# Issuing TensorE's matmuls block by block, and outer-product units that use all four row quadrants, in a fused attention and MLP backward kernel

## The chip, the cores and the metric

One core of a Trainium2 chip. The metric is the device time of one execution in microseconds (us). Executions of one kernel scatter; each is fast or slow (slow: more than 1.5% above the fastest of the same kernel), and ratios use fast runs alone.

## The reference

One token for two sequences goes through a layer norm, then in parallel through attention over a cache (32 query heads, 16 key and value heads, 4096 positions, head size 128) and a bilinear MLP (576 to 4608 and back). The function returns the output and all gradients. What matters here are the two largest of these, the gradients of the caches, each of the shape of the cache:

```python
def _fwd_reference(A_x, A_k_cache, A_v_cache, A_wq, A_wo, B_x, B_w_gate, B_w_up, B_w_down):
    # [...] _A_ref: scores = q k^T * Dh**-0.5, softmax, p v, times wo;  _B_ref: (x w_gate) * (x w_up) w_down
    x = A_x
    xn = _layernorm(x, axis=-1)
    return x + _A_ref(xn, A_k_cache, A_v_cache, A_wq, A_wo) + _B_ref(xn, B_w_gate, B_w_up, B_w_down)

def reference(...):            # [...]
    _out, _vjp = jax.vjp(_f, A_x, A_k_cache, A_v_cache, A_wq, A_wo, B_w_gate, B_w_up, B_w_down)
    return (_out, *_vjp(grad_out))
```

With one query position, the gradient of a cache row is a rank-one product: a row of 4096 numbers (probabilities, or gradients of scores) times a vector of 128. So the kernel reads 92 MB, writes 92 MB, and TensorE (PE) does many small matmuls.

## The kernel before

A framework records the instructions, and its scheduler decides at build time in which order they stand on each engine; PE ran its list in that order (its changes of array shape, counted in the traces and in the orders as built, are the same 683 before and 1010 after). PE uses its array in three shapes here: whole (128 rows x 128 columns, the scores), column tiles (128 x 32, contractions and the small MLP products), and row tiles (32 x 128, the outer products, whose contracted dimension is 32 rows of one row quadrant).

```python
    def ps_o():                                   # a pair tile, in two halves; two such tiles exist
        return ps.tile([P, 2, 512], FP32, tag="o", bufs=2, name="ps_o")

    def head_scores(n, t, x, s_ps, half):         # 16 whole-array matmuls on one half of a head
        # [...] a 32x32 transpose of half a head on DVE into X
        for e in range(2):
            be = 2 * half + e
            for c8 in range(8):
                nc.tensor.matmul(s_ps[:], lhsT=view(W[t][:], ...), rhs=view(X[:], ...), start=..., stop=...)

    def outer_units(rows, bd, b, l0, oview):      # gradients of two cache heads: 8 units, 256 in all
        def unit(x, ch, A):
            def f():
                # [...]
                o = ps_o()
                for c in range(4):
                    for aa in range(2):
                        a = 2 * A + aa            # row quadrant: 0 and 1, or 2 and 3
                        nc.tensor.matmul(o[:, aa, c * Dh:(c + 1) * Dh], lhsT=rows[32 * a:32 * a + 32, 4 * ch + c, :],
                                         rhs=bd[32 * a:32 * a + 32, x * Dh:(x + 1) * Dh], start=True, stop=True)
                evac(st[:, 2 * A:2 * A + 2, 4 * ch:4 * ch + 4, :].rearrange(...), o[:], 1024)
                # [...] the last unit of a head issues its 1 MB output DMA
            return f
        return [unit(x, ch, A) for x in range(2) for ch in range(2) for A in range(2)]
```

`evac` copies a tile from PSUM to SBUF as bf16, on ACT or DVE by a running account of their loads. The main loop mixes these units with the work on the next heads and with units of the MLP.

## Time and profile before

| | before |
|---|---|
| time, median of the first 3 runs | 550.38 us |
| PE, DVE, ACT busy (profiled run, slow, 560.2 us) | 475.7, 362.0, 330.6 us |
| mean granted clock of PE (profiled run; fast runs of later calls 0.78 to 0.82) | 0.766 |
| read and written | 92.48 and 92.48 MB |
| changes of array shape, in PE's order | 654 |

"Busy" of PE counts the modelled duration of every matmul; overlapping ones count once. Distances between starts say more, and the prediction works with them. The lines of the profile are shown there. The granted clock in the traces of the kernel before and of the changed one is either full (1.0) or half (0.5), and each record of it but the cut-off last lasts a whole multiple of 3.413 us, the shortest 3.413 us; a stretch of that length is called a window here, and the kernel before has 80 of them at full clock and 76 at half.

### The profile page before, as it was taken

To read this page: it belongs to the slowest core of one execution; us is meant where nothing else is said; L and a number is where in the kernel's file an instruction comes from. 1 tells how busy PE (TensorE), PEld (TensorE's weight loads), DVE (VectorE), ACT (ScalarE), POOL (GpSimd) and SP (SyncE) were. 2 spreads that over 40 slices of the span, in tenths; PEclk is the share of its full clock that TensorE was granted. 3 is DMA by queue.
4 is the path that set the end of the run, shared out by engine and by line. 5 is a ranking of instruction groups with operands and counts; after the bars stand their busy time and mean duration, and the time that the engine had idled before them with its cause. 6 is when DMAs were issued, how large, how long until landed. Compare 5 with 4: busy or idle time off the path is not lost.

```text
span 560.2 us, 20059 instructions
## 1 busy us (share of the span) xinstructions
PE 475.7 (85%) x8921; PEld 362.5 (65%) x8921; DVE 362.0 (65%) x624; ACT 330.6 (59%) x454; POOL 204.6 (37%) x372
## 2 busy tenths in 40 slices
PE   0588988998989999888989899998888999879873
PEld 0476766776776677666767667776776757767630
DVE  8685655757657646458575675668676646577564
ACT  1135695857566465567565665667555566566553
POOL 5125252432622521624235243344243243351322
PEclk9988798877787555688787975589888566798955
DMA  8993999999699998699997999979979889764546
GB/s 254 411 385 135 355 412 368 397 381 405 227 403 393 384 366 324 213 388 379 353 391 253 417 415 375 393 279 411 392 294 390 356 291 403 283 239 171 219 152 245
DMA packets 52911, 186.26 MB, mean 333 GB/s; under 512 B 4140, under 2 KB 19128, under 8 KB 44632
## 3 DMA queue, kind: packets, MB, share of 16 engines
q1 hardware_dynamic: 28392, 92.49, 44.3%
q0 software_dynamic: 24432, 92.48, 43.0%
q8 instruction: 70, 1.15, 0.8%
q14 instruction: 17, 0.14, 0.1%
HBM read 92.48 MB, written 92.48 MB: 330 GB/s over the span
## 4 chain that ended last, share of the span: by engine, by line
PE 31%; ACT 9%; issue 5%; DVE 4%; POOL 2%; POOLq 0%; DVEq 0%; ACTq 0%
PE ps_sc L503 11%; ACT so L93 8%; PE ps_o L549 6%; PE ps_m L518 4%; PE ps_m L527 1%; POOL prm L533 1%; PE ps_m L440 1%; PE ps_o L681 1%; DVE so L90 1%; PE ps_o L651 1%; DVE sto L90 1%; PE ps_m L272 1%; PE ps_o L364 1%; PE ps_m L618 1%; DVE X L102 1%
## 5 line engine op out<-in xcount | busy, mean ns | idle before, releaser
L93 ACT CAST so<-ps_o 128x1024 bf16<-128x1024 f32 x232 | 225.1, 1019 | 125.5 <-PE ps_o L549 114.0
L503 PE MATMUL ps_sc<-X,W 128*128 128x128 bf16 x2048 | 197.2, 249 | 5.3 <-DVE X L102 4.5
L102 DVE STREAM_TRANSPOSE X<-kv 128x1024 f32<-128x1024 f32 x128 | 157.6, 1233 | 44.1 <-PE ps_sc L503 42.7
L503 PEld LDWEIGHTS <-W 128*128 128x128 bf16 x2048 | 153.1, 112 | 27.7 <-issue 17.5
L553 POOL DMA_DIRECT2D out_dram<-so x64 | 50.0, 781 | 138.5 <-ACT so L93 74.6
L549 PE MATMUL ps_o<-bd,dsm 32*128 32x128 bf16 x1024 | 50.9, 245 | 10.3 <-ACT so L93 5.8
L518 PE MATMUL ps_m<-kv,rowT 128*32 128x128 bf16 x2048 | 59.3, 272 | 0.0
L549 PE MATMUL ps_o<-bd,prm 32*128 32x128 bf16 x1024 | 46.3, 250 | 14.3 <-POOL prm L533 7.0
L518 PEld LDWEIGHTS <-rowT 128*32 128x32 bf16 x2048 | 43.0, 121 | 10.0 <-issue 5.8
L549 PEld LDWEIGHTS <-dsm 32*128 32x128 bf16 x1024 | 30.4, 104 | 24.8 <-issue 18.4
L549 PEld LDWEIGHTS <-prm 32*128 32x128 bf16 x1024 | 27.8, 105 | 26.8 <-issue 13.5
L533 POOL TENSOR_TENSOR prm<-pr,maskc 128x1024 bf16<-128x1024 bf16 x16 | 30.2, 1888 | 36.5 <-DVE pr L580 36.5
L93 ACT CAST stw<-ps_o 128x1024 bf16<-128x1024 f32 x28 | 27.8, 1028 | 13.8 <-PE ps_o L364 12.6
L474 POOL COPY dM<-qd 128x128 bf16<-128x128 bf16 x32 | 9.3, 289 | 73.1 <-PE ps_m L480 46.2
L90 DVE CAST so<-ps_o 128x1024 bf16<-128x1024 f32 x24 | 29.1, 1211 | 8.7 <-PE ps_o L549 8.2
L467 POOL COPY W<-rep 32x16 bf16<-32x16 bf16 x128 | 24.7, 193 | 26.1 <-PE ps_sc L503 18.9
L533 POOL TENSOR_TENSOR dsm<-ds,maskc 128x1024 bf16<-128x1024 bf16 x16 | 30.2, 1889 | 4.6 <-DVE ds L600 4.0
L93 ACT CAST std<-ps_o 128x576 bf16<-128x576 f32 x36 | 22.8, 646 | 12.6 <-PE ps_o L397 12.4
L102 DVE STREAM_TRANSPOSE Xw<-wgu 128x1152 f32<-128x1152 f32 x18 | 24.5, 1360 | 4.1 <-PE ps_sc L503 4.0
L93 ACT CAST sto<-ps_o 128x576 bf16<-128x576 f32 x25 | 15.6, 642 | 14.1 <-PE ps_o L681 13.9
L719 DVE TENSOR_SCALAR oT<-ps_m 128x4 bf16<-128x4 f32 x16 | 2.7, 171 | 29.6 <-PE ps_m L527 29.6
L371 POOL DMA_DIRECT2D out_dram<-stw x18 | 13.5, 752 | 19.0 <-ACT stw L93 10.6
(178 smaller groups left out, 591.8 us busy)
## 6 DMA issues: line engine op xcount, KB each, us to landing
out_dram<-so POOLq DMA_DIRECT2D x64, 1024.0 KB, 9.5
kv<-in_A_k_cache_dram SPq DMA_DIRECT2D x32, 1024.0 KB, 11.8
kv<-in_A_v_cache_dram SPq DMA_DIRECT2D x32, 1024.0 KB, 10.1
out_dram<-stw POOLq DMA_DIRECT2D x18, 512.0 KB, 9.3
wd<-in_B_w_down_dram SPq DMA_DIRECT2D x9, 576.0 KB, 12.7
out_dram<-std POOLq DMA_DIRECT2D x9, 576.0 KB, 7.9
wo<-in_A_wo_dram SPq DMA_DIRECT2D x4, 1152.0 KB, 13.4
wgu<-in_B_w_gate_dram SPq DMA_DIRECT2D x9, 512.0 KB, 14.0
```

Of the source, the lines that this page charges most:

```text
L90: nc.vector.tensor_copy(out=out, in_=in_)
L93: nc.scalar.copy(out, in_)
L102: nc.vector.transpose(out, in_)
L272: nc.tensor.matmul(dp[32 * gq:32 * gq + 32, 0:P], lhsT=view(Wm[:], 0, P, 8 * pos(q, s), [[1, 32]]), rhs=view(X[:], 0, P, koff(s) * 256 + ( ...
L371: nc.gpsimd.dma_start(out[0:512, f0:f0 + FS].rearrange("(c p) n -> p c n", p=P), st[:])
L467: nc.gpsimd.tensor_copy(view(W[t][:], 32 * a, 32, 28 + 32 * a, [[2 * WW, 4], [WW + 2, 2], [1, 2]]), view(st["rep"][:], 32 * a, 32, t * 4 * ...
L474: nc.gpsimd.tensor_copy(view(dM[:], 0, P, t * 2 * P, [[P + 2, 2], [4, 32], [1, 2]]), view(st["qd"][:], 0, P, (2 if t == 0 else 1) * GH * 2 ...
L503: nc.tensor.matmul(s_ps[:], lhsT=view(W[t][:], 0, P, (be * 2 + x) * WW + 28 - 4 * c8, [[1, P]]), rhs=view(X[:], 0, P, c8 * 64 + e, [[8 * 6 ...
L518: nc.tensor.matmul(o_ps[32 * cg:32 * cg + 32, :], lhsT=view(rowsT[:], 0, P, c4 * 32 + 4 * c8, [[1, 32]]), rhs=head[:, 8 * c4 + c8, :], sta ...
L533: nc.gpsimd.tensor_tensor(m[:], view(rows[:], 0, P, 0, [[0, 8], [1, P]]), view(maskc[:], 0, P, 0, [[1, 8], [0, P]]), ALU.mult)
L549: nc.tensor.matmul(o[:, aa, c * Dh:(c + 1) * Dh], lhsT=rows[32 * a:32 * a + 32, 4 * ch + c, :], rhs=bd[32 * a:32 * a + 32, x * Dh:(x + 1) ...
L553: nc.gpsimd.dma_start(oview[b, :, :, l0 + x].rearrange("a m n -> m a n"), st[:].rearrange("p a c d -> p a (c d)"))
```

## The change

The intent is that PE runs one product after the other without a break, and that an outer-product unit keeps all four row quadrants at work. A class `Block` wraps each loop of matmuls. In the units of the caches, two units become one that fills both pair tiles, with the quadrants in the order 2, 0, 3, 1; the calls that hand out units are halved. Cut to its core:

```diff
+    class Block:
+        def __init__(self):
+            self.first, self.stack = None, ExitStack()
+        def __enter__(self):
+            return self
+        def __call__(self, *args, **kwargs):
+            ins = nc.tensor.matmul(*args, **kwargs)
+            if self.first is None:
+                self.first = ins
+                self.stack.enter_context(tc.issue_after(ins.ins))
+                self.stack.enter_context(tc.high_priority())
+        def __exit__(self, *exc):
+            self.stack.close()
 [...]
-        for e in range(2):
-            be = 2 * half + e
-            for c8 in range(8):
-                nc.tensor.matmul(
+        with Block() as mm:
+            for e in range(2):
+                be = 2 * half + e
+                for c8 in range(8):
+                    mm(
 [... the same around fifteen other loops of matmuls ...]
-        def unit(x, ch, A):
+        def unit(x, ch):
 [...]
-                o = ps_o()
-                for c in range(4):
-                    for aa in range(2):
-                        a = 2 * A + aa
-                        nc.tensor.matmul(o[:, aa, c * Dh:(c + 1) * Dh], lhsT=rows[32 * a:32 * a + 32, 4 * ch + c, :],
-                                         rhs=bd[32 * a:32 * a + 32, x * Dh:(x + 1) * Dh], start=True, stop=True)
-                evac(st[:, 2 * A:2 * A + 2, 4 * ch:4 * ch + 4, :].rearrange("p a c d -> p a (c d)"), o[:], 1024)
+                o = [ps_o(), ps_o()]
+                with Block() as mm:
+                    for c in range(4):
+                        for a in (2, 0, 3, 1):
+                            mm(o[a // 2][:, a % 2, c * Dh:(c + 1) * Dh], lhsT=rows[32 * a:32 * a + 32, 4 * ch + c, :],
+                               rhs=bd[32 * a:32 * a + 32, x * Dh:(x + 1) * Dh], start=True, stop=True)
+                for A in range(2):
+                    evac(st[:, 2 * A:2 * A + 2, 4 * ch:4 * ch + 4, :].rearrange("p a c d -> p a (c d)"), o[A][:], 1024)
```

`issue_after` only says that an instruction stands somewhere behind the block's first one on PE. `high_priority()` without a number sets the scheduler's count back to 0 for what is recorded inside.

More of the change, by code (lines that the diff above doesn't have):

```diff
@@ L268, in dxn @@
             dve(1.4)
-            for r in range(4):
-                for gq in range(4):
-                    q, s = 2 * half + gq // 2, 4 * (gq % 2) + r
-                    nc.tensor.matmul(
-                        dp[32 * gq:32 * gq + 32, 0:P], lhsT=view(Wm[:], 0, P, 8 * pos(q, s), [[1, 32]]),
-                        rhs=view(X[:], 0, P, koff(s) * 256 + (2 * (q % 2) + (s // 2) % 2) * 64 + s % 2,
-                                 [[kstep * 256, 4], [2, 32]]),
-                        start=(r == 0), stop=(r == 3))
-            for r in range(2):
-                for gq in range(4):
-                    q, s = 2 * half + gq // 2, 2 * (gq % 2) + r
-                    nc.tensor.matmul(
-                        dp[32 * gq:32 * gq + 32, P:160], lhsT=view(Wt[:], 0, P, 8 * (4 * q + s), [[1, 32]]),
-                        rhs=view(X[:], 0, P, 8 * 256 + (2 * (q % 2) + s // 2) * 64 + s % 2, [[2, 32]]),
-                        start=(r == 0), stop=(r == 1))
+            with Block() as mm:
+                for r in range(4):
+                    for gq in range(4):
+                        q, s = 2 * half + gq // 2, 4 * (gq % 2) + r
+                        mm(
+                            dp[32 * gq:32 * gq + 32, 0:P], lhsT=view(Wm[:], 0, P, 8 * pos(q, s), [[1, 32]]),
+                            rhs=view(X[:], 0, P, koff(s) * 256 + (2 * (q % 2) + (s // 2) % 2) * 64 + s % 2,
+                                     [[kstep * 256, 4], [2, 32]]),
+                            start=(r == 0), stop=(r == 3))
+            with Block() as mm:
+                for r in range(2):
+                    for gq in range(4):
+                        q, s = 2 * half + gq // 2, 2 * (gq % 2) + r
+                        mm(
+                            dp[32 * gq:32 * gq + 32, P:160], lhsT=view(Wt[:], 0, P, 8 * (4 * q + s), [[1, 32]]),
+                            rhs=view(X[:], 0, P, 8 * 256 + (2 * (q % 2) + s // 2) * 64 + s % 2, [[2, 32]]),
+                            start=(r == 0), stop=(r == 1))
             nc.vector.tensor_add(accx[:], accx[:], dp[:])
@@ L302, in gate_up @@
             ug = ps_m([P, 2, P])
-            for w in range(2):
-                for dc in range(5):
-                    k = 4 * w + dc if dc < 4 else 8
-                    for a in range(4):
-                        nc.tensor.matmul(ug[32 * a:32 * a + 32, 1 - w, :], lhsT=xs[:, dc if dc < 4 else 4 + w, :],
-                                         rhs=wgu[:, k, P * a:P * (a + 1)], start=(dc == 0), stop=(dc == 4))
+            with Block() as mm:
+                for w in range(2):
+                    for dc in range(5):
+                        k = 4 * w + dc if dc < 4 else 8
+                        for a in range(4):
+                            mm(ug[32 * a:32 * a + 32, 1 - w, :], lhsT=xs[:, dc if dc < 4 else 4 + w, :],
+                                             rhs=wgu[:, k, P * a:P * (a + 1)], start=(dc == 0), stop=(dc == 4))
             m["gs"] = gs = sb.tile([P, 2, P], FP32, tag="gs", bufs=1, name="gs")
@@ L317, in down @@
             dh = ps_m([P, FC * 32])
-            for k in range(NB):
-                for e in range(2):
-                    nc.tensor.matmul(
-                        dh[:], lhsT=Wdy[:, k, e, :], rhs=view(Xd[:], 0, P, 64 * k + e, [[D, FC], [2, 32]]),
-                        start=(k == 0 and e == 0), stop=(k == NB - 1 and e == 1),
-                    )
+            with Block() as mm:
+                for k in range(NB):
+                    for e in range(2):
+                        mm(
+                            dh[:], lhsT=Wdy[:, k, e, :], rhs=view(Xd[:], 0, P, 64 * k + e, [[D, FC], [2, 32]]),
+                            start=(k == 0 and e == 0), stop=(k == NB - 1 and e == 1),
+                        )
             m["hb"] = hb = sb.tile([P, 3, P], BF16, tag="hb", bufs=2, name="hb")
@@ L343, in grads @@
             yp = ps_m([P, 5, 2])
-            for dc in range(5):
-                for c in range(FC):
-                    nc.tensor.matmul(yp[:, dc, :], lhsT=wd[:, c, DOFF[dc]:DOFF[dc] + P], rhs=hT[:, c, 0:2],
-                                     start=(c == 0), stop=(c == FC - 1))
+            with Block() as mm:
+                for dc in range(5):
+                    for c in range(FC):
+                        mm(yp[:, dc, :], lhsT=wd[:, c, DOFF[dc]:DOFF[dc] + P], rhs=hT[:, c, 0:2],
+                                         start=(c == 0), stop=(c == FC - 1))
             nc.vector.tensor_add(acc[:], acc[:], yp[:])
@@ L360, in f @@
                 o = ps_o()
-                for dc in range(4):
-                    for aa in range(2):
-                        a = 2 * A + aa
-                        nc.tensor.matmul(o[:, aa, dc * P:(dc + 1) * P],
-                                         lhsT=xnr[32 * a:32 * a + 32, dc * P:(dc + 1) * P],
-                                         rhs=hb[32 * a:32 * a + 32, 1 + w, :], start=True, stop=True)
+                with Block() as mm:
+                    for dc in range(4):
+                        for aa in range(2):
+                            a = 2 * A + aa
+                            mm(o[:, aa, dc * P:(dc + 1) * P],
+                                             lhsT=xnr[32 * a:32 * a + 32, dc * P:(dc + 1) * P],
+                                             rhs=hb[32 * a:32 * a + 32, 1 + w, :], start=True, stop=True)
                 evac(view(st[:], 0, P, 256 * A, [[P, 2], [FS, 4], [1, P]]),
@@ L378, in outer_tail @@
                 o = ps_o()
-                for w in range(2):
-                    for aa in range(2):
-                        a = 2 * A + aa
-                        nc.tensor.matmul(o[64 * w:64 * w + 64, aa, 0:P], lhsT=xnr[32 * a:32 * a + 32, 512:576],
-                                         rhs=hb[32 * a:32 * a + 32, 1 + w, :], start=True, stop=True)
+                with Block() as mm:
+                    for w in range(2):
+                        for aa in range(2):
+                            a = 2 * A + aa
+                            mm(o[64 * w:64 * w + 64, aa, 0:P], lhsT=xnr[32 * a:32 * a + 32, 512:576],
+                                             rhs=hb[32 * a:32 * a + 32, 1 + w, :], start=True, stop=True)
                 evac(st[:, 256 * A:256 * A + 256].rearrange("p (a f) -> p a f", a=2), o[:, :, 0:P], 256)
@@ L394, in f @@
                 o = ps_o()
-                for aa in range(2):
-                    a = 2 * A + aa
-                    nc.tensor.matmul(o[:, aa, 0:HD2], lhsT=hb[32 * a:32 * a + 32, 0, :],
-                                     rhs=dyr[32 * a:32 * a + 32, k * HD2:(k + 1) * HD2], start=True, stop=True)
+                with Block() as mm:
+                    for aa in range(2):
+                        a = 2 * A + aa
+                        mm(o[:, aa, 0:HD2], lhsT=hb[32 * a:32 * a + 32, 0, :],
+                                         rhs=dyr[32 * a:32 * a + 32, k * HD2:(k + 1) * HD2], start=True, stop=True)
                 evac(st[:, 2 * A:2 * A + 2, k * HD2:(k + 1) * HD2], o[:, :, 0:HD2], D)
@@ L422, in group_front @@
         qp = ps_m([P, GH, 2])
-        for h in range(GH):
-            for dc in range(5):
-                if dc < 4:
-                    l, r = wq[:, 2 * dc + h // 4, (h % 4) * P:(h % 4 + 1) * P], xs[:, dc, 0:2]
-                else:
-                    l, r = wq[:, 8, (h % 4) * P:(h % 4 + 1) * P], xs[:, 4 + h // 4, 0:2]
-                nc.tensor.matmul(qp[:, h, :], lhsT=l, rhs=r, start=(dc == 0), stop=(dc == 4))
+        with Block() as mm:
+            for h in range(GH):
+                for dc in range(5):
+                    if dc < 4:
+                        l, r = wq[:, 2 * dc + h // 4, (h % 4) * P:(h % 4 + 1) * P], xs[:, dc, 0:2]
+                    else:
+                        l, r = wq[:, 8, (h % 4) * P:(h % 4 + 1) * P], xs[:, 4 + h // 4, 0:2]
+                    mm(qp[:, h, :], lhsT=l, rhs=r, start=(dc == 0), stop=(dc == 4))
         nc.vector.tensor_copy(qd[:, 0], qp[:])
@@ L437, in group_front @@
                 pairs(wo[:, 4 * half:4 * half + 4].rearrange("p c n -> p (c n)")))
-            for k in range(NB):
-                for e in range(2):
-                    nc.tensor.matmul(
-                        do_ps[:, P * half:P * half + P], lhsT=Wdy[:, k, e, :],
-                        rhs=view(Xo[:], 0, P, 64 * k + e, [[D, 4], [2, 32]]),
-                        start=(k == 0 and e == 0), stop=(k == NB - 1 and e == 1),
-                    )
+            with Block() as mm:
+                for k in range(NB):
+                    for e in range(2):
+                        mm(
+                            do_ps[:, P * half:P * half + P], lhsT=Wdy[:, k, e, :],
+                            rhs=view(Xo[:], 0, P, 64 * k + e, [[D, 4], [2, 32]]),
+                            start=(k == 0 and e == 0), stop=(k == NB - 1 and e == 1),
+                        )
         dof = sb.tile([P, GH, 32], FP32, tag="dof", bufs=1, name="dof")
@@ L499, in head_scores @@
         dve(1.2)
-        for e in range(2):
-            be = 2 * half + e
-            for c8 in range(8):
-                nc.tensor.matmul(
-                    s_ps[:], lhsT=view(W[t][:], 0, P, (be * 2 + x) * WW + 28 - 4 * c8, [[1, P]]),
-                    rhs=view(X[:], 0, P, c8 * 64 + e, [[8 * 64, 4], [2, 32]]),
-                    start=(x == 0 and be == 0 and c8 == 0), stop=(x == 1 and be == 3 and c8 == 7),
-                )
+        with Block() as mm:
+            for e in range(2):
+                be = 2 * half + e
+                for c8 in range(8):
+                    mm(
+                        s_ps[:], lhsT=view(W[t][:], 0, P, (be * 2 + x) * WW + 28 - 4 * c8, [[1, P]]),
+                        rhs=view(X[:], 0, P, c8 * 64 + e, [[8 * 64, 4], [2, 32]]),
+                        start=(x == 0 and be == 0 and c8 == 0), stop=(x == 1 and be == 3 and c8 == 7),
+                    )
     def contract(rowsT, heads):
         o_ps = ps_m([P, Dh])
-        for c4 in range(4):
-            for c8 in range(8):
-                for x, head in enumerate(heads):
-                    cg = 2 * x + c8 % 2
-                    nc.tensor.matmul(
-                        o_ps[32 * cg:32 * cg + 32, :],
-                        lhsT=view(rowsT[:], 0, P, c4 * 32 + 4 * c8, [[1, 32]]),
-                        rhs=head[:, 8 * c4 + c8, :],
-                        start=(c4 == 0 and c8 < 2), stop=(c4 == 3 and c8 > 5))
+        with Block() as mm:
+            for c4 in range(4):
+                for c8 in range(8):
+                    for x, head in enumerate(heads):
+                        cg = 2 * x + c8 % 2
+                        mm(
+                            o_ps[32 * cg:32 * cg + 32, :],
+                            lhsT=view(rowsT[:], 0, P, c4 * 32 + 4 * c8, [[1, 32]]),
+                            rhs=head[:, 8 * c4 + c8, :],
+                            start=(c4 == 0 and c8 < 2), stop=(c4 == 3 and c8 > 5))
         o_sb = sb.tile([P, Dh], FP32, tag="o_sb", bufs=1, name="o_sb")
@@ L538, in outer_units @@
         m = {}
-        def unit(x, ch, A):
+        def unit(x, ch):
             def f():
-                if ch == 0 and A == 0:
+                if ch == 0:
                     m["st"] = stile([P, 4, 8, Dh], "so")
                 st = m["st"]
-                o = ps_o()
-                for c in range(4):
-                    for aa in range(2):
-                        a = 2 * A + aa
-                        nc.tensor.matmul(o[:, aa, c * Dh:(c + 1) * Dh], lhsT=rows[32 * a:32 * a + 32, 4 * ch + c, :],
-                                         rhs=bd[32 * a:32 * a + 32, x * Dh:(x + 1) * Dh], start=True, stop=True)
-                evac(st[:, 2 * A:2 * A + 2, 4 * ch:4 * ch + 4, :].rearrange("p a c d -> p a (c d)"), o[:], 1024)
-                if ch == 1 and A == 1:
+                o = [ps_o(), ps_o()]
+                with Block() as mm:
+                    for c in range(4):
[4 more added lines that the diff above has]
+                    evac(st[:, 2 * A:2 * A + 2, 4 * ch:4 * ch + 4, :].rearrange("p a c d -> p a (c d)"), o[A][:], 1024)
+                if ch == 1:
                     nc.gpsimd.dma_start(oview[b, :, :, l0 + x].rearrange("a m n -> m a n"),
@@ L555, in unit @@
             return f
-        return [unit(x, ch, A) for x in range(2) for ch in range(2) for A in range(2)]
+        return [unit(x, ch) for x in range(2) for ch in range(2)]
     def softmax(s_ps):
@@ L615, in first @@
             yp = ps_m([P, 5, 2])
-            for dc in range(5):
-                for h in range(GH):
-                    nc.tensor.matmul(yp[:, dc, :], lhsT=wo[:, h, DOFF[dc]:DOFF[dc] + P], rhs=oT[:, 0, h, 0:2],
-                                     start=(h == 0), stop=(h == GH - 1))
+            with Block() as mm:
+                for dc in range(5):
+                    for h in range(GH):
+                        mm(yp[:, dc, :], lhsT=wo[:, h, DOFF[dc]:DOFF[dc] + P], rhs=oT[:, 0, h, 0:2],
+                                         start=(h == 0), stop=(h == GH - 1))
             nc.vector.tensor_add(acc[:], acc[:], yp[:])
@@ L646, in f @@
                 o = ps_o()
-                for dc in range(2):
-                    for aa in range(2):
-                        a = 2 * A + aa
-                        d0 = (2 * k + dc) * P
-                        nc.tensor.matmul(o[:, aa, 256 * dc:256 * dc + 256], lhsT=xnr[32 * a:32 * a + 32, d0:d0 + P],
-                                         rhs=R[32 * a:32 * a + 32, 1].rearrange("p h d -> p (h d)"),
-                                         start=True, stop=True)
+                with Block() as mm:
+                    for dc in range(2):
+                        for aa in range(2):
+                            a = 2 * A + aa
+                            d0 = (2 * k + dc) * P
+                            mm(o[:, aa, 256 * dc:256 * dc + 256], lhsT=xnr[32 * a:32 * a + 32, d0:d0 + P],
+                                             rhs=R[32 * a:32 * a + 32, 1].rearrange("p h d -> p (h d)"),
+                                             start=True, stop=True)
                 evac(view(st[:], 0, P, 512 * A, [[256, 2], [GH * P, 2], [1, 256]]),
@@ L665, in outer_qt @@
                 o = ps_o()
-                for aa in range(2):
-                    a = 2 * A + aa
-                    nc.tensor.matmul(o[64 * A:64 * A + 64, aa, 0:256], lhsT=xnr[32 * a:32 * a + 32, 512:576],
-                                     rhs=R[32 * a:32 * a + 32, 1].rearrange("p h d -> p (h d)"), start=True, stop=True)
+                with Block() as mm:
+                    for aa in range(2):
+                        a = 2 * A + aa
+                        mm(o[64 * A:64 * A + 64, aa, 0:256], lhsT=xnr[32 * a:32 * a + 32, 512:576],
+                                         rhs=R[32 * a:32 * a + 32, 1].rearrange("p h d -> p (h d)"), start=True, stop=True)
                 evac(st[64 * A:64 * A + 64].rearrange("p (a n) -> p a n", a=2), o[64 * A:64 * A + 64, :, 0:256], 512)
@@ L678, in f @@
                 o = ps_o()
-                for aa in range(2):
-                    a = 2 * A + aa
-                    nc.tensor.matmul(o[:, aa, 0:HD2], lhsT=R[32 * a:32 * a + 32, 0, h2, :],
-                                     rhs=dyr[32 * a:32 * a + 32, k * HD2:(k + 1) * HD2], start=True, stop=True)
+                with Block() as mm:
+                    for aa in range(2):
+                        a = 2 * A + aa
+                        mm(o[:, aa, 0:HD2], lhsT=R[32 * a:32 * a + 32, 0, h2, :],
+                                         rhs=dyr[32 * a:32 * a + 32, k * HD2:(k + 1) * HD2], start=True, stop=True)
                 evac(view(m["so"][:], 0, P, h2 * D + k * HD2, [[2 * D, 2], [1, HD2]]), o[:, :, 0:HD2], D)
@@ L708, in slot @@
         head_scores(n, t, l % 2, s_ps, 0)
-        more(2)
+        more(1)
         if mid:
@@ L712, in slot @@
         head_scores(n, t, l % 2, s_ps, 1)
-        more(2)
+        more(1)
         other(per)
@@ L855 @@
     while outs or side:
-        more(2)
+        more(1)
         other(1)
```

## The prediction

> **What bounds the kernel now.** I read the page first (busy shares, the slices, the waits), then the waits of TensorE (PE), then its timeline in two stretches, and last the order in which the instructions of both programs stand on PE.
>
> ```profile
> PE 475.7 (85%) x8921; PEld 362.5 (65%) x8921; DVE 362.0 (65%) x624; ACT 330.6 (59%) x454; POOL 204.6 (37%) x372
> PE   0588988998989999888989899998888999879873
> PEclk9988798877787555688787975589888566798955
> DMA  8993999999699998699997999979979889764546
> ```
>
> The reader is to see that PE is the busiest engine, that outside the first slice and the last it is 80 to 90% busy nearly everywhere, and that its granted clock is a mixture: 5 is a slice wholly at half clock. DMA is close behind (9 in most slices). The profile fell in the slow state (560.2 us against a median of 550.38), so I use it for durations and not for the total.
>
> The waits of PE are small. The largest that belongs to the parts changed is this one:
>
> ```profile
> PE ps_o L549 <- ACT so L93: 11.7, 27, 0.8
> ```
>
> PE waited 11.7 us in all, in 27 places, for an outer product's PSUM tile to be emptied. ACT on the other side waited 114.0 us for PE's outer products (the page's first group). So PE sets the pace, not the eviction. DVE and ACT have a third of the span free.
>
> What PE spends its time on is seen in its timeline. First a stretch at half clock, then one at full clock (columns: start us, duration us, engine, line, operation, tiles, shapes, count):
>
> ```profile
> 350.33 0.82 PE L503 MATMUL ps_sc<-X,W 128*128 128x128 bf16 x6
> 351.08 0.61 PE L364 MATMUL ps_o<-hb,xnr 32*128 32x128 bf16 x8
> 351.62 0.82 PE L503 MATMUL ps_sc<-X,W 128*128 128x128 bf16 x6
> ...
> 355.82 0.63 PE L549 MATMUL ps_o<-bd,dsm 32*128 32x128 bf16 x16
> 356.38 0.37 PE L562 MATMUL ps_m<-identf,mx 128*1 128x128 f32 x1
> ```
>
> ```profile
> 370.38 0.40 PE L549 MATMUL ps_o<-bd,prm 32*128 32x128 bf16 x8
> 370.70 0.91 PE L518 MATMUL ps_m<-kv,rowT 128*32 128x128 bf16 x52
> ...
> 376.12 0.42 PE L549 MATMUL ps_o<-bd,prm 32*128 32x128 bf16 x16
> 376.47 0.29 PE L480 MATMUL ps_m<-ident,dM 128*128 128x128 bf16 x2
> 376.60 1.08 PE L503 MATMUL ps_sc<-X,W 128*128 128x128 bf16 x16
> 377.62 0.40 PE L549 MATMUL ps_o<-bd,dsm 32*128 32x128 bf16 x8
> ```
>
> Take differences of starts. At full clock the 16 score matmuls take 1.02 us, which is 15 steps of 57 ns and one step of 149 ns to the first matmul of another array shape. At half clock 6 take 0.75 us: 5 steps of 107 ns and one of about 240. Over the whole trace the medians are the same: 57 and 107 ns between score matmuls, 144 to 160 ns (full) and 238 to 246 ns (half) for a step between two array shapes (32 rows, 32 columns, whole), 266 ns for the step from 32 columns to 32 rows at full clock. So **a change of shape costs about 90 ns more at full clock and 135 ns more at half clock than staying.** Eight outer matmuls of two row quadrants take 0.32 us (full) and 0.54 us (half) with the step out; sixteen, of four quadrants, take 0.35 and 0.56 us. Sixteen cost what eight cost: that is the gain that the change is after. But the kernel before already has it often: the scheduler put two units together.
>
> [...]
>
> **The change part by part.**
> (1) *Blocks in one piece.* The first matmul of a block is queued first, the others must come after it and have a raised priority. Nothing ties them to each other, so two raised blocks can alternate. The order of the changed program shows both outcomes. Score blocks of exactly 16 go from 31 to 82, contractions of 64 from 17 to 27: this is the intent. But there are also 39 stretches of at least six runs of three matmuls or fewer (503 runs in all), where the order before has none: one outer matmul, two score matmuls, one outer matmul, and so on, usually in the second half of an outer block. **The changes of array shape rise from 654 to 978.**
> (2) *Four quadrants side by side.* In the order before, 79 runs of outer products have 16 matmuls and 59 have 8. In the new one 57 have 16 and 87 have 8, and 227 stand alone. The second pair tile comes free later than the first, so the scheduler issues the eight matmuls for the tile that is free, and then lets the other eight into another block. The gain of four quadrants is not won for more than half of the units.
> (3) Evictions: 256 of cache outer products as before (232 on ACT, 24 on DVE in both programs), same size. Output DMAs: same number and size. No time here.
>
> Sum for PE. I multiply each program's runs by the durations above (57 or 107 ns a whole-array step, about 25 for a two-column one, 13.6 or 25 a column-tiled one, runs of 8 and 16 outer matmuls 184/299 and 212/325 ns from first to last, and the steps between shapes). Before: 343 us if all were at full clock, 576 us if all were at half. After: 388 and 642. The part for changes of shape alone goes from 107 to 157 us at full clock and from 160 to 238 at half; matmuls inside runs go down by 2 to 5 us and the few same-shape steps by 3 to 6. So **PE gets 45 us more work at full clock, 66 at half.**
>
> Before, 76 windows of 3.413 us at half clock (259 us) hold 259/576 = 45% of the work; the other 55% need 0.55 x 343 = 189 us. That is 448 us of issuing; the remaining 102 of 550 are the start (some 37 us), the tail (some 15) and waits (some 50).
>
> The clock: one outer matmul and two score matmuls take 147+149+57 = 353 ns at full clock[...]; at half clock 589 ns[...]. [...] I take the work done at half clock as 50% in place of 45%: 0.5 x 388 + 0.5 x 642 = 515 us. Of the 50 us of waits a busier PE hides perhaps 15 to 20. 515 + 102 - 20 = 597 us.
>
> **The rivals.**
> (a) *The longer blocks raise the clock and win.* [...] With 35% at half clock: 0.65 x 388 + 0.35 x 642 = 477, with 85 of the rest 562 us; only at 30% is the time before reached. Against it: the alternating stretches lie all through the order[...].
> (b) *The extra shape changes fall into waits and cost nothing.* The halves of an outer block part because the second tile is still being emptied, and ACT needs 1.02 us for one. For it: PE has waits of some 50 us. Against it: only 11.7 us of these are for the tile that ACT empties, and the score matmuls between were work that PE had anyway. If the whole 45 to 66 us were hidden, 550 us.
> (c) *ACT becomes the bound.* A pair of tiles takes 2.04 us on ACT, and PE fills it only when both are empty, so ACT stands for some 0.4 to 0.6 us per pair. 128 pairs x 2.6 = 333 us, and the other evictions and copies some 100 us: 430 us, under the time. Only locally would this add waits, at most 20 us: 617 us.
> (d) *DMA hides it.* 186.26 MB at the 403 to 417 GB/s of the best slices are 447 to 462 us; a slower PE relieves DMA. No time.
>
> **Range and chances.** From 40% at half clock with 15 us of waits more hidden (0.6 x 388 + 0.4 x 642 = 490, + 72 = 562) to 58% with the waits as they were (535 + 97 = 632). Predicted 597 us, 562 to 632. Faster by over 2% would need rival (a) in full: 0.04. Within 2% needs (a) or (b) in large part: 0.08. Slower: 0.88.
>
> **What would show it.** In the profile after: shape changes near 980 in PE's order of time; alternating single outer matmuls and pairs of scores with steps of 150 or 240 ns; a mean granted clock a little lower than before; PE's busy share at 85% or more and ACT's and DVE's busy times unchanged in us, at a lower share; the wait of ACT for outer products longer than 114.0 us. The prediction is wrong if the clock is clearly higher, if steps into and out of a single outer matmul take much less than 140 ns, or if idle time of PE falls by as much as the changes of shape add.

## The result, and the profile after

The changed kernel took **607.34 us** in the median (601.12 to 616.61, 4 runs), the kernel before in all its 4 runs 553.31 us (550.19 to 558.83). The ratio of the fast runs is **1.096**, 95% interval 1.081 to 1.111. (A ratio is the mean time of one kernel's fast runs over that of the other's of the same rounds, so it is not quite the ratio of the medians quoted.) The outputs are right.

The page of the changed kernel (a fast run of 608.39 us), its engines' busy times and the slices of the granted clock:

```profile
span 606.6 us, 20079 instructions
PE 525.3 (87%) x8921; PEld 384.6 (63%) x8921; DVE 357.8 (59%) x624; ACT 331.3 (55%) x454; POOL 204.1 (34%) x372
PEclk9999597665659576589659957769665599777655
```

PE has the same 8921 matmuls and is busy 525.3 us in place of 475.7. ACT and DVE have the same work in us (331.3 after 330.6, 357.8 after 362.0), at a lower share of the span. PE's idle time, span less busy, is 81.3 us after 84.5: it did not take up the added work. So the added time is time in which PE is at work, as far as a profile from a slow run before and one from a fast run after can be compared.

The waits of the changed kernel, the two that answer to those in the prediction (matmuls now all carry the line of the block's helper, L93):

```profile
ACT so L112 <- PE ps_o L93: 141.0, 104, 6.5
PE ps_o L93 <- ACT so L112: 13.2, 30, 1.1
```

ACT waits longer for PE (141.0 us after 114.0). PE waits for ACT hardly longer than before (13.2 after 11.7).

PE's timeline shows what PE does with its time. A stretch at full clock:

```profile
190.10 0.29 PE L93 MATMUL ps_sc<-X,W 128*128 128x128 bf16 x2
190.32 0.23 PE L93 MATMUL ps_o<-bd,dsm 32*128 32x128 bf16 x1
190.48 0.29 PE L93 MATMUL ps_sc<-X,W 128*128 128x128 bf16 x2
190.70 0.22 PE L93 MATMUL ps_o<-bd,dsm 32*128 32x128 bf16 x1
190.86 0.29 PE L93 MATMUL ps_sc<-X,W 128*128 128x128 bf16 x2
191.08 0.22 PE L93 MATMUL ps_o<-bd,dsm 32*128 32x128 bf16 x1
```

and one at half clock:

```profile
253.26 0.39 PE L93 MATMUL ps_sc<-X,W 128*128 128x128 bf16 x2
253.59 0.28 PE L93 MATMUL ps_o<-bd,prm 32*128 32x128 bf16 x1
253.80 0.39 PE L93 MATMUL ps_sc<-X,W 128*128 128x128 bf16 x2
254.13 0.28 PE L93 MATMUL ps_o<-bd,prm 32*128 32x128 bf16 x1
```

Each turn of one outer matmul and two score matmuls takes 0.38 us at full clock and 0.54 us at half clock. Eight turns at full clock take 3.0 us; they hold eight outer matmuls and 16 score matmuls, which take 0.32 and 1.02 us, 1.3 us together, where each kind stands in one run. In the order of time PE changes the shape of its array 1010 times in this trace; in that of the kernel before 683 times (here each matmul counts by its own tile size, and the programs' orders then give the same 1010 and 683; the 978 and 654 used elsewhere count some small matmuls with a larger shape, which lowers these two by about 30 and those of the other versions by 7 to 43). At half clock are 93 of 169 windows of 3.413 us; before 76 of 156.

### The profile page after: what moved, and what is told of

Read it like the earlier page. It is cut to its first block, busy times and chain, and to the rows that moved or that the text cites. A ratio compares the mean times of both kernels' runs of the same rounds, so it can differ in the third digit from the quotient of the medians.

```text
span 606.6 us, 20079 instructions
## 1 busy us (share of the span) xinstructions
PE 525.3 (87%) x8921; PEld 384.6 (63%) x8921; DVE 357.8 (59%) x624; ACT 331.3 (55%) x454; POOL 204.1 (34%) x372
## 5 line engine op out<-in xcount | busy, mean ns | idle before, releaser
L112 ACT CAST so<-ps_o 128x1024 bf16<-128x1024 f32 x232 | 226.0, 1016 | 148.1 <-PE ps_o L93 141.0
L93 PE MATMUL ps_sc<-X,W 128*128 128x128 bf16 x2048 | 215.2, 254 | 10.6 <-DVE X L121 6.0
L93 PEld LDWEIGHTS <-W 128*128 128x128 bf16 x2048 | 156.9, 113 | 38.3 <-issue 13.8
L93 PE MATMUL ps_o<-bd,dsm 32*128 32x128 bf16 x1024 | 79.4, 260 | 11.0 <-ACT so L112 5.5
L93 PE MATMUL ps_o<-bd,prm 32*128 32x128 bf16 x1024 | 75.1, 252 | 8.7 <-ACT so L112 4.6
L93 PEld LDWEIGHTS <-dsm 32*128 32x128 bf16 x1024 | 40.8, 107 | 38.9 <-issue 25.3
L93 PEld LDWEIGHTS <-prm 32*128 32x128 bf16 x1024 | 37.2, 104 | 36.0 <-issue 21.3
L93 PE MATMUL ps_m<-kv,rowT 128*32 128x128 bf16 x2048 | 47.6, 254 | 0.4 <-issue 0.2
L93 PEld LDWEIGHTS <-rowT 128*32 128x32 bf16 x2048 | 38.3, 114 | 4.5 <-issue 2.0
L112 ACT CAST stw<-ps_o 128x1024 bf16<-128x1024 f32 x28 | 28.1, 1018 | 18.5 <-PE ps_o L93 13.2
L93 PEld LDWEIGHTS <-Wdy 128*128 128x128 bf16 x306 | 26.3, 124 | 6.4 <-POOL dM L503 3.1
L555 ACT COPY o_sb<-ps_m 128x128 f32<-128x128 f32 x32 | 8.7, 270 | 24.0 <-PE ps_m L93 23.9
```

What stands on the lines that cost most here:

```text
L93: ins = nc.tensor.matmul(*args, **kwargs)
L112: nc.scalar.copy(out, in_)
L555: nc.scalar.copy(o_sb[:], o_ps[:])
```

## The experiments

The theory (A): the time comes from changes of array shape on PE; they come from two raised blocks that alternate, because each block's priorities start again from 0; the alternation needs the two-tile unit, whose second tile comes free late, while another block is under way. The rivals: (B) the two tiles of a unit, which must both be empty, cost waits; (C) the raised priority holds up the short steps of the softmax chain. Each version's order on PE is known when it is built, so its PE steps can be summed as in the prediction before it runs. In the table, "steps" is 0.55 times the sum at full clock plus 0.45 times the sum at half clock, less the same for the kernel before (448 us); "measured" is the ratio of fast runs less one, times 550 us.

| run | changes of shape | outer matmuls alone | steps, us | median, us | ratio | measured, us |
|---|---|---|---|---|---|---|
| before | 654 | 3 | 0 | 550 to 554 | 1 | 0 |
| the change | 978 | 227 | +54 | 607.34 | 1.096 | +53 |
| blocks_only | 460 | 0 | -33 | 524.96 | 0.949 | -28 |
| pair_only | 706 | 2 | +11 | 555.97 | 1.014 | +8 |
| off2000 | 558 | 8 | -10 | 529.31 | 0.955 | -25 |
| after_so_off | 468 | 0 | -27 | 535.59 | 0.973 | -15 |
| after_only_so | 664 | 0 | +2 | 546.79 | 0.992 | -5 |
| after_sc_off | 763 | 83 | +19 | 548.19 | 0.988 | -6 |
| after_o0123 | 1119 | 277 | +73 | 630.82 | none, one fast run | |
| zero128 | 448 | 0 | -16 | 532.0 | 0.958 | -23 |
| zero32 | 960 | 0 | +40 | 592.89 | 1.064 | +35 |
| anchor2 | 499 | 63 | -20 | 588.97 | 1.061 | +33 |
| blocks_only_5 | 460 | 0 | -33 | 520.76 | 0.938 | -34 |
| after_so_off_5 | 468 | 0 | -27 | 537.37 | 0.960 | -22 |

The outputs of all runs are right. The runs came after that of the change, each with its own runs of the kernel before.

### One part at a time

**blocks_only**: the blocks of the change, with the units of the kernel before.

```diff
-        def unit(x, ch):
-                o = [ps_o(), ps_o()]
-                        for a in (2, 0, 3, 1):
+        def unit(x, ch, A):
+                o = ps_o()                              # one pair tile, 8 matmuls, two quadrants
+                        for aa in range(2):             # [... inside a Block, as in the change ...]
 [...]
-        more(1)
+        more(2)                                         # at all three places
```

> The blocks as in the change, but the cache outer units as before (one pair tile each). Its order has 460 changes of array shape (654 before, 978 in the change) and no outer matmul that stands alone; the sum of PE's steps is 316 us at full and 535 us at half clock (before 343 and 576). Theory A (the added time is PE's changes of shape, which come from two raised blocks that alternate): 45% at half clock gives 415 us, with some 100 us of rest 515 to 525 us, faster than before. Theory B (the two pair tiles of a unit, which must both be empty, are the cause): about the time before, 545 to 555 us. Theory C (raised blocks hold up the latency chain of softmax and the other small steps): 590 us or more.

Measured: 524.96 us, ratio 0.949 (0.930 to 0.968). The blocks by themselves make the kernel *faster*, as the sum of steps says. C falls: it expected 590 us or more. B is not tested here, since no unit has two tiles.

**pair_only**: the units of the change, without any block.

```diff
-                self.stack.enter_context(tc.issue_after(ins.ins))
-                self.stack.enter_context(tc.high_priority())
```

> The two-tile units without any block. 706 changes of shape, steps of 352 us at full and 589 us at half clock. Theory A: 459 us of steps at 45% half clock and 100 us of rest, about 560 us, within 1 to 3% of before. Theory B: close to the changed kernel, 595 us or more. Theory C: the time before, 550 us.

Measured: 555.97 us, ratio 1.014 (1.004 to 1.025). The two-tile units alone cost 1.4%. So the change's two parts are worth -28 and +8 us, and +53 us together: the loss is in their meeting.

### What meets

**off2000**: the change with one word more.

```diff
-                self.stack.enter_context(tc.high_priority())
+                self.stack.enter_context(tc.high_priority(offset=2000))
```

> The change with one edit: the raised priority of a block is its own minus 2000 in place of a count from 0 in every block, so that of two blocks under way the older always goes first. 558 changes of shape, 8 outer matmuls alone in place of 227, steps of 335 and 563 us. Theory A: 437 + 100 = about 537 us. Theory B and C: the two-tile units and the raised blocks are all still there, so 590 us or more.

Measured: 529.31 us, ratio 0.955 (0.941 to 0.970). Now each block's priority is its place in the program less 2000, so of two blocks the older one goes first until it is done. Single outer matmuls fall from 227 to 8. The two-tile units are all still there, so having them is not enough for the loss; PE waits 14.8 us for a tile that ACT empties, against 13.2 us in the change. The blocks are still raised, though by 2000 places and no longer to the start, so against C it is blocks_only that weighs, where they are raised as far as in the change. It is even 15 us better than the steps say; the clock is probably part of it (0.841 and 0.812 in its fast runs, against 0.79 to 0.82 before), as the sum keeps 45% at half clock for all.

**after_so_off**: the change, the cache units no longer raised.

```diff
-                with Block() as mm:                       # in unit(x, ch) alone
+                with Block(False) as mm:                  # False: neither issue_after nor high_priority
```

> The change, but the cache outer units are not blocks (their matmuls have the normal priority); they still fill two tiles, and all other blocks stand. 468 changes of shape, no outer matmul alone, steps of 321 and 542 us: by PE's order alone the same as the run with blocks only. Theory A: 415 to 420 us of steps, some 520 us. Theory B: 590 us or more. If it is slower than the run with blocks only by over 10 us, the two tiles have a cost of their own beside the order.

Measured: 535.59 us, ratio 0.973 (0.962 to 0.985). Again a gain. It lies some 10 us over the run with blocks only (531 to 541 us against 518 to 528), with 5 to 7 us of it in the steps.

**after_only_so**: the reverse, the cache units as the only raised blocks (`Block(False)` everywhere else).

> The change with the cache outer units as the only raised blocks; all other matmuls have the normal priority. With one kind of raised block there is nothing of the same priority to alternate with: no outer matmul stands alone, 664 changes of shape (before 654), steps of 345 us at full and 578 us at half clock (before 343 and 576). Theory A: like the kernel before, 548 to 562 us. Theory that raising the outer units is in itself what costs (they push the score blocks and the eviction engines out of step): 590 us or more.

Measured: 546.79 us, ratio 0.992 (0.983 to 1.001). Raising one kind of block alone neither alternates nor costs. It takes two raised kinds.

**after_sc_off**: all raised except the score blocks.

> The change with all blocks raised except the score blocks. The outer units can alternate with the other kinds only: 83 outer matmuls alone, 763 changes of shape, steps of 361 us at full and 597 us at half clock. Theory A: 472 us of steps at 47% half clock and some 95 us of rest, 560 to 575 us, between the kernel before and the change.

Measured: 548.19 us, ratio 0.988 (0.977 to 0.999). **A miss**: 560 to 575 us were expected. Two of its four runs are slow (555.63 and 552.39 us). The profiled one has this busy line, over a span of 553.7 us:

```profile
PE 482.6 (87%) x8921; PEld 364.3 (66%) x8921; DVE 359.4 (65%) x624; ACT 330.1 (60%) x454; POOL 206.1 (37%) x372
```

PE is idle 71.1 us here against 84.5 in the kernel before, both in slow runs: some 13 us of the added 19 went into time in which PE had waited. The rest of the miss is left open. So rival (b) of the prediction, changes of shape that fall into waits, is real at this size; with 324 added changes it was not seen.

### More of it, and by itself

**after_o0123**: a dose. The same instructions, the quadrants in another order.

```diff
-                        for a in (2, 0, 3, 1):
+                        for a in (0, 1, 2, 3):
```

> A dose: the changed kernel with its four quadrants issued in the order 0, 1, 2, 3 in place of 2, 0, 3, 1. Same instructions, same tiles, same evictions; the scheduler now alternates more: 1119 changes of shape (978), 277 outer matmuls alone (227), steps of 401 and 667 us (388 and 642). Theory A: about 20 us slower than the change, 615 to 635 us. Theory B (the two tiles' wait) and C (the raised priority): the change's 607 us, within 8.

Measured: 630.82 us in the median; its one fast run took 619.94 us, 14 us over the median of the change's fast runs (606.29), and its three slow ones 630.1 to 634.64 us, 14 to 18 us over the change's slow run (616.61). The steps say 18. (The two ran in different calls, with the kernel before at 554.46 and 553.31 us.) More alternation, more time, with every tile, eviction and priority rule the same.

**zero128 and zero32**: the cost of a change of shape by itself. On the kernel with blocks only, two matmuls with zero weights are put into each score block. They add exact zeros to the scores, so the outputs stay right. PE's order is line by line the same in both; in one the zero matmuls use all 128 rows, in the other 32.

```diff
+    zw = const.tile([P, P], BF16, name="zw")
+    nc.vector.memset(zw[:], 0.0)
 [... in head_scores, inside the block ...]
+                    if c8 == 3:
+                        mm(s_ps[:], lhsT=zw[0:128, :], rhs=X[0:128].rearrange("p c d -> p (c d)")[:, 0:P],   # zero32: 0:32
+                           start=False, stop=False)
```

> Control for the next run, on the kernel with blocks only (524.96 us): two matmuls with zero weights, of all 128 rows, are added inside each of the 128 score blocks of 16 (256 in all; they add zeros to the scores, the result stays right). No added change of shape (448 in the order). Theory A: 256 x 57 to 107 ns = 15 to 27 us of steps at most; [...] 520 to 540 us.

> The same 256 zero matmuls at the same places (PE's order is the same line by line), but of 32 rows, so each brings two changes of array shape: 512 more. Theory A: 256 x (149 + 147 - 2 x 57) = 47 us more than the control at full clock, 256 x (241 + 241 - 2 x 107) = 69 us more at half, and a lower clock: 575 to 600 us. If changes of shape are hidden in waits or cost nothing beside a matmul's own step, the two runs are the same within 10 us.

Measured: 532.0 us (ratio 0.958) and 592.89 us (ratio 1.064), 61 us apart. The same place in PE's timeline, first with 128 rows, then with 32, both at full clock:

```profile
131.08 0.39 PE L93 MATMUL ps_sc<-X,W 128*128 128x128 bf16 x4
131.31 0.22 PE L93 MATMUL ps_sc<-X,zw 128*128 128x128 bf16 x1
131.36 0.62 PE L93 MATMUL ps_sc<-X,W 128*128 128x128 bf16 x8
131.83 0.22 PE L93 MATMUL ps_sc<-X,zw 128*128 128x128 bf16 x1
131.88 0.39 PE L93 MATMUL ps_sc<-X,W 128*128 128x128 bf16 x4
```

```profile
131.08 0.39 PE L93 MATMUL ps_sc<-X,W 128*128 128x128 bf16 x4
131.40 0.23 PE L93 MATMUL ps_sc<-X,zw 32*128 32x128 bf16 x1
131.56 0.63 PE L93 MATMUL ps_sc<-X,W 128*128 128x128 bf16 x8
132.12 0.23 PE L93 MATMUL ps_sc<-X,zw 32*128 32x128 bf16 x1
132.28 0.40 PE L93 MATMUL ps_sc<-X,W 128*128 128x128 bf16 x4
```

The smaller matmul costs more. From the start of the score matmul before it to the start of the one after it are 112 ns in the median with 128 rows and 306 ns with 32 (full clock), 208 and 456 ns at half clock. So a change of shape costs 97 ns more than a step within one shape at full clock and 124 ns at half (the prediction took 92 and 134). 183 x 194 + 73 x 248 ns, by the clock at which each of the 256 fell, make 54 us, near the 61, but the match hides two more terms. The pages, 128 rows first:

```profile
PE 420.6 (79%) x9177; PEld 339.3 (64%) x9177; DVE 361.1 (68%) x625; ACT 327.7 (62%) x454; POOL 204.8 (39%) x372
PE 505.9 (86%) x9177; PEld 368.3 (62%) x9177; DVE 363.2 (61%) x625; ACT 329.6 (56%) x454; POOL 204.9 (35%) x372
```

With 32 rows PE is busy 85 us more and idle 24 us less (85.1 in place of 108.7). So some 31 us beyond the 54 were added, probably by the clock (73 windows at half clock against 37), and 24 us fell into waits; no run separates these two.

**anchor2**: a unit that starts only when both its tiles are free.

```diff
-            if self.first is None:
+            self.n += 1
+            if self.n == self.heads:                      # heads = 2 for the cache units, else 1
                 self.first = ins
```

> The change, but the outer block's other matmuls are queued behind its second matmul, so that 14 of 16 go only when both tiles are free. 499 changes of shape, no outer run of 8, steps of 327 and 552 us. Theory A: 410 to 420 us of steps and 105 to 110 of rest, since a unit now waits for both tiles: 520 to 540 us. Theory B: about 600 us, since the wait for two tiles is even stricter than in the change.

Measured: 588.97 us, ratio 1.061 (1.054 to 1.067). **A miss**, and on the side of rival B. Its page:

```profile
span 588.0 us, 20079 instructions
PE 434.0 (74%) x8921; PEld 343.2 (58%) x8921; DVE 358.6 (61%) x624; ACT 331.2 (56%) x454; POOL 204.7 (35%) x372
```

and the largest of PE's waits (us in total, times, longest):

```profile
PE ps_o L93 <- ACT so L113: 46.7, 61, 1.3
```

PE's busy time is 42 us lower than before, but PE is idle for 154 us in place of 84.5, and 46.7 us of its idle time are waits for a cache tile that ACT empties (11.7 before). The score blocks are whole, and PE, whose list is fixed, stands before the second matmul of a unit until ACT is done. The other half of the added idle time is spread over smaller waits. Rival B's mechanism exists. That in the changed kernel the scheduler fills this wait with another block, and so pays in changes of shape instead, is read from its short waits (13.2 us) and its order; no run shows it by itself.

### The fastest version

> The version with blocks only once more, with five rounds, for a clear verdict as the fastest of all versions: 520 to 530 us, 4 to 6% below the kernel before.

> The two-tile units, not raised, with all other blocks, once more on the same chip with five rounds. By PE's steps it equals the run with blocks only (321 and 542 us against 316 and 535, so 5 to 7 us more); what it takes beyond that is the cost of a unit that needs two tiles. 530 to 540 us; 10 us over the other as in the first look, or equal if that was scatter.

Measured on one chip: blocks only 520.76 us (514.84 to 529.0, 6 runs), ratio 0.938 (0.930 to 0.945); with two-tile units that are not raised 537.37 us (528.35 to 541.31), ratio 0.960 (0.951 to 0.968). No run of the first is as slow as any of the 11 runs of the kernel before beside it (548.31 to 563.68). The 10 us between the two were not scatter: the fast runs' means are 518.5 (four runs) and 529.2 us (two). 5 to 7 us of the 10.7 are steps; what the rest is stays open, since the two versions differ both in the tiles of a unit and in whether the cache units are raised.

The version with blocks only beats both kernels. Its page, with the granted clock:

```profile
PE 415.7 (80%) x8921; PEld 332.8 (64%) x8921; DVE 360.0 (69%) x624; ACT 327.5 (63%) x454; POOL 204.7 (39%) x372
PEclk9989998969557777997787997998897799999755
```

and a piece of PE's timeline:

```profile
207.95 1.08 PE L93 MATMUL ps_sc<-X,W 128*128 128x128 bf16 x16 [0.62 <-DVE X L121]
208.96 0.25 PE L93 MATMUL ps_o<-hb,xnr 32*64 32x128 bf16 x4
209.14 0.40 PE L93 MATMUL ps_o<-bd,dsm 32*128 32x128 bf16 x8
209.47 0.27 PE L594 MATMUL ps_m<-identf,mx 128*1 128x128 f32 x1
209.64 1.08 PE L93 MATMUL ps_sc<-X,W 128*128 128x128 bf16 x16
210.65 0.43 PE L93 MATMUL ps_o<-bd,dsm 32*128 32x128 bf16 x16
```

Score blocks are whole here, and the outer products stand in eights and sixteens: without two-tile units the scheduler still puts two units side by side 103 times. PE is busy 415.7 us, and 100 of 144 windows have the full clock.

## Why the prediction was right

It put 597 us, 562 to 632, with 88% on slower; 607.34 us were measured.

- *PE is the bound.* Right: PE's busy time rose by 50 us and the span by 46 (slow profile before, fast one after), with ACT's and DVE's work unchanged.
- *Blocks alternate, changes of shape rise by 324.* Right: 327 more in the trace (683 to 1010). The reason it gave, that nothing ties a block's matmuls to each other, is half of it. The run off2000 shows the other half: the count of priorities that starts at 0 in every block.
- *A change of shape costs 90 and 135 ns.* Nearly: 97 and 124 ns where it was isolated. At that price the 324 added changes are 31 to 40 us (an estimate); the rest of the 53 us would be the lower clock, which no run held fixed. In the changed kernel the step out of a single outer matmul took 157 ns at full clock (147 assumed) and 215 ns at half (242 assumed).
- *45 us more at full clock, 66 at half; 50% of the work at half clock.* The step from 45 to 50% was the author's estimate; what sets the clock was not shown. Right by the count of windows: 93 windows of 3.413 us are 317 us, and 317/642 is 49%. With it the steps are 513 us (515 predicted), though this uses the sum at half clock of the prediction. Too much by the traces, as the point on waits shows.
- *Four quadrants side by side are won too seldom.* Right: the changed order has 57 runs of 16 where the one before had 79, and pair_only is no faster than before. Two tiles are not needed for it: in the order before, 76 of the 79 runs of 16 are eight matmuls on quadrants 0 and 1 and then eight on 2 and 3, from two units, and they are as good as parallel (208 ns from first start to last at full clock, against 190 ns for the changed kernel's runs of 16).
- *A busier PE hides 15 to 20 us of waits.* **This is the term that was mis-sized.** PE's idle time went from 84.5 (in a slow run) to 81.3 us, so 3 us were hidden. The added work was put too high as well. Summed over the two traces (distances between starts, idle time taken out), the steps are 453 us before and 502 after, 49 more, where the prediction has 448 and 515, 67 more. At half clock stand 237 us of steps before and 279 after, 41% and 43% of the work (of 576 and 642 us), not 45 and 50: the windows at half clock also hold waits, which the prediction counted as work. The two errors, 18 us in the work and 17 in the waits, cancel, and that is luck: the predicted rise of 47 us meets the 46 us between the two profiles. Between fast runs the rise is 53 us; how its terms divide stays open, since no fast run of the kernel before was profiled.
- *The granted clock is a little lower.* Right: 0.735 to 0.758 in the fast runs after, 0.78 to 0.82 in fast runs before. The 45% before came from a slow profile; the clocks of fast runs, some 0.80, mean 40% of the time at half clock, 0.4 x 548/576 = 38% of the work. The prediction's rest of 102 us was then some 15 us too small. The errors of the two levels cancel in the difference only in part, which is why the table's "steps" are to be read to 10 or 15 us.
- *Slips in the working.* The upper end takes 97 us for waits "as they were", where the rest was 102 us (637 us in all). The 102 itself takes steps from the slow profile off a median of 550; off the profile's own 560 it would be 112. The 266 ns from 32 columns to 32 rows seems to hold waits: the 42 such steps at full clock took 108 to 1020 ns, and the 16 of them without idle time have a median of 152 ns. None of them changes the direction.
- *Rival (a), that long blocks raise the clock and win,* was judged improbable for the change, and rightly; but the blocks alone do win (-6.2%), with clocks of 0.81 to 0.88; their fewer changes of shape give -33 us in the table, so how much the clock adds is open. *Rival (c)*, waits for two tiles, is not what the change pays, but anchor2 shows that it is what a stricter block would pay.

## What to carry to other kernels

Before running a change that reorders work, read the order that the scheduler built: count the changes of PE's array shape and price each at the step measured in the trace of the kernel before; here this came within 15 us, with two exceptions: a new wait (anchor2, 53 us off) and added changes that cost no time (after_sc_off, 25 us off). Priorities that start from the same value in every group can make two groups alternate one by one; use one that keeps the groups in order. And a unit that needs two buffers at once is harder to place than two units that need one each, and here it gains next to nothing over two such units that stand side by side.

## What was measured of TensorE

- A change of array shape, measured with the zero matmuls, took 97 ns at full clock and 124 ns at half over a step of 56 or 104 ns within one shape. A 32-row matmul between whole-array ones cost 194 ns (306 against 112) at full clock and 248 ns (456 against 208) at half more than one of 128 rows in its place.
- The clock was half in a stretch in which PE had no break. In the kernel before PE is busy 26.98 of 27.00 us and has half the clock throughout:

```profile
342.00:369.00 27.00, 26.98 (x380) 20.49 (x380) 13.87 (x20) 16.61 (x24) 10.64 (x16) 0.50 0.95 359
```

  (the columns are the stretch, its length, busy us and counts of PE, PEld, DVE, ACT and POOL, granted clock, DMA share, GB/s). What sets the clock was not shown. The clock of fast runs was 0.86 to 0.88 with 256 zero whole-array matmuls, and 0.77 to 0.80 with 32-row ones at the same places.
- Eight matmuls of 128 columns on two row quadrants took 0.32 us and sixteen on four 0.35 us at full clock, where the second eight stood directly behind the first eight or between them (208 and 190 ns from first start to last). Where two score matmuls stood between single outer ones, eight turns took 3.0 us in place of 1.3.
